# The first matrix of one chunk by seven products on half chunks, on one Trainium2 core

## The chip, the core and the metric

The kernel runs on one core of a Trainium2 chip. The time is the device time of one execution in microseconds. The engines are named as in the profile: PE is TensorE's matmul, PEld its weight load, DVE is VectorE, ACT is ScalarE, POOL is GpSimd, and SP is the engine that issues nearly all transfers (DMAs).

## The reference

```python
# attention: 8 x 8 heads, 576 positions, 64 columns; heads 0 to 3 see the last 32 positions,
# heads 4 to 7 every fourth of the last 128
scores = np.where(masks, scale * np.matmul(q, k.T), -1e9)
attn = np.exp(scores - max); attn = attn / (sum(attn) + 1e-09)
x = np.matmul(attn, v) as (4608 tokens, 512)
# feed-forward
h = x @ w_in                                            # 512 -> 2048
g = np.maximum(h, 0.0) + np.log1p(np.exp(-np.abs(h)))   # softplus
out = g @ w_out                                         # 2048 -> 512
```

All in float32. Each float32 factor is split in a high part, which TensorE multiplies exactly, and a low part, the rest; a product is three matmuls: high by high, high by low, low by high.

## The kernel before

The 4608 tokens are nine chunks of 512. Their inputs x come from attention, which runs for couples of head pairs ahead of the chunk: a visit to PE for the scores, softmax on ACT and DVE, a transposition of 32x32 squares by a way through DRAM, a second visit for the weighted values, and a second way through DRAM that brings x (x_full).

Chunks 0, 1 and 2 are computed directly, in 48 slots (`RUNS`, L43: six slots of chunk 0, ten of chunk 1, ten of 0, six of 1, then all sixteen of chunk 2). A slot is one block of 128 of the 2048 hidden columns: 12 matmuls of 512 columns make its h (`h_part`, L667: 4 blocks of the 512 inputs by three part products, from the weight tile `wt[ff, 0]`), ACT takes the absolute value, exp and ln of it and DVE the maximum (L682 to L689), a cast and a subtraction split it (gh, gl), and two slots later 12 matmuls add it to the four output banks (`o_unit`, L1192; `LAG`, L59).

Chunks 3 to 8 are computed in three pairs ("supers") by Strassen's and Winograd's scheme: both matrices are seen as 2x2 blocks and each 2x2 product is done by seven products instead of eight (`PRODUCTS`, L810), on blocks of one whole chunk (512 columns). The scheme needs sums of blocks on both sides: of x (`x_before`, L996: s1 to s4) and of weights (`job`, L1080: t1 to t4 of one pair of weight tiles p and one matrix i). A job makes its sums on POOL or DVE, splits them, and writes them to DRAM (`streamed`), from where the supers load them into a ring of five tiles. Before, three jobs of the first matrix are done in chunk 0 or 1, seven more jobs during chunk 2, and the last six in the first super.

PE's order is fixed by the order in which `on_tensor` is called, attention visits excepted. Everything else is ordered by a list planner (`planned`, L1471): each task has a cost, a latest time, and a due-time offset from two tables by task number (`HURRIED`, L60, in us, and `CHOSEN`, L68, the engine where there is a choice). At run time each engine works strictly in the order the planner wrote. A tile is used again only once its readers are done, DMAs among them.

Of the kernel before, what the change touches and what calls it, by code (L numbers as in the profile page):

```python
# [53 lines left out]
LATE_JOBS = 6  # L54
# [12 lines left out]
}  # L67
CHOSEN = {  # L68
    295: "ACT", 467: "DVE", 535: "DVE", 554: "DVE", 586: "DVE", 595: "DVE", 819: "DVE", 853: "DVE", 865: "DVE",
    868: "DVE", 882: "DVE", 885: "DVE", 888: "DVE", 901: "DVE", 903: "DVE", 905: "ACT", 908: "DVE", 1210: "DVE",  # L70
    1213: "DVE", 1219: "DVE", 1238: "DVE", 1266: "DVE", 1281: "DVE", 1307: "DVE", 1322: "DVE", 1336: "DVE",
    1345: "DVE", 1580: "DVE", 1670: "DVE", 1676: "DVE", 1694: "DVE", 1716: "DVE", 1731: "DVE", 1767: "DVE",
    1772: "DVE", 1777: "DVE", 2010: "DVE", 2042: "DVE", 2094: "DVE", 2112: "DVE",
# [41 lines left out]
def tile_windowed_attention_softplus_ffn(  # L115
# [22 lines left out]
    opened = const.tile([P, 704], F32, name="opened", tag="k2")  # L138
# [133 lines left out]
    still = opened[:, 448:].bitcast(BF16)  # L272
# [22 lines left out]
    def x_half(c, k):  # L295
        if (c, k) not in x_full:
            turn = k if c < PLAIN else 2 * ((c - PLAIN) % 2) + k
            x_full[c, k] = const.tile([P, 2, CH], F32, name="x_full", tag=f"x_{'abcd'[turn]}")
        return x_full[c, k]
# [412 lines left out]
    def ob_tiles(c, resumed=False):  # L712

        tags = ("w13_0", "w14_0") if c == FIRST else ("x_c", "x_d") if c or not resumed else ("g_x", "g_y", "xl01")
# [106 lines left out]
    def keep_block(i, p, b):  # L821
# [6 lines left out]
        "a11": ("w0_0", "w1_0"), "s2": ("w4_0", "w5_0"), "a12": ("w2_0", "w3_0"), "s3": ("w6_0", "w7_0"),  # L828
        "s1": ("w8_0", "w9_0"), "a22": ("w0_1", "w1_1"), "s4": ("w2_1", "w3_1"),
# [166 lines left out]
    def x_before(c, name):  # L996
        first = c == PLAIN
        if name[0] == "s":
            others = {"s1": ["a22"], "s2": ["s1"], "s3": ["a22", "s2"], "s4": ["s2"]}[name]
            sum_task(1024, x_sum, c, name, reads=[X_KEY[n] for n in others], writes=[X_KEY[name]])  # L1000
        at_home = [k for tag in X_HOMES[name] for k in home_keys(tag)] if first else []
        cast_task(1024, lambda: x_high(c, name), reads=[X_KEY[name]], writes=[("xh", name), *at_home])
        task("DVE", 1024, x_low, c, name, reads=[X_KEY[name], ("xh", name)], writes=[("xl", name)], port=True)
# [13 lines left out]
    def weights(n, begun=False):  # L1017
        x = x_of_couple(n)
        queries = ["q0", "q1"] if begun else [x]
        if not begun:  # L1020
            transfer(load_queries, n, writes=queries, size=TILE, n=2)
# [43 lines left out]
    jobs = {}  # L1065

    def job_tiles(stage):
        if stage not in jobs:
# [7 lines left out]
            tags = (("x_c", "x_d"), ("xl10", "xl11"), ("n3", "n4"))[stage]  # L1076
            jobs[stage] += [tile_at(tag, "cast", F32R, (P, 2, 2, HALF)) for tag in tags]
        return jobs[stage]

    def job(i, p, stage):  # L1080
# [4 lines left out]
        else:  # L1085
            key = [("a", 0), ("a", 1), ("a", 2)]
            key += [("x1", "l", 0), ("x1", "l", 1)] if stage else [("x", 1, 0), ("x", 1, 1)]
            tile_keys = key[:3] if stage == 0 else []
            tile_keys += key[3:]
# [25 lines left out]
        def high(n):  # L1115
            return job_tiles(late)[3 + n][:, :, 0], of(n)

        def low(n):
            dst = job_tiles(late)[3 + n]
# [4 lines left out]
        def keep(n):  # L1124
            for m, b in enumerate(("t2", "t4") if n else ("t1", "t3")):
                load_dma(out=streamed[i, b, p // 2][:, p % 2], in_=job_tiles(late)[3 + n][:, m].bitcast(F32))
# [49 lines left out]
    def early_slot(i):  # L1176
# [9 lines left out]

    OB_KEYS = {
        "kept": [("x", 1, 0), ("x", 1, 0), ("x", 1, 1), ("x", 1, 1)], 0: [("gx",), ("gy",), ("x0", "l", 1), ("x0", "l", 1)],
        1: [("x", 1, 0), ("x", 1, 0), ("x", 1, 1), ("x", 1, 1)], 2: [("W", 13, 0), ("W", 13, 0), ("W", 14, 0), ("W", 14, 0)],
    }  # L1190

    def o_unit(i):  # L1192
# [7 lines left out]
        for m in range(NKT):  # L1200
# [3 lines left out]
        if not final:  # L1204
            return
# [211 lines left out]
    last_resumed = slots.index((2, 0)) + LAG  # L1417
    for i in range(PLANNED, LAST + 1):
        if i == kept_first + 1:
            for n in range(FIRST_JOBS):  # L1420
                sooner(job, JOBS_SOONER)(n // NPAIR, n % NPAIR, 0)
        if slots[i] == (2, 0):
            for k in range(2):
                cast_task(1024, lambda k=k: x_half_high(2, k), reads=[("x", 0, k)], writes=[("x0", "h", k)])
                task(
                    "DVE", 1024, x_half_low, 2, k, reads=[("x", 0, k), ("x0", "h", k)], writes=[("x0", "l", k)], port=True
                )
# [228 lines left out]
```

## Time and profile before

| | |
|---|---|
| median of three executions | 818.75 us (816.95 to 819.33) |
| the profiled execution | 819.88 us, its span 818.1 us |
| PE busy | 801.9 us, 98% of the span |
| DVE busy | 660.2 us, 81% |
| ACT busy | 501.8 us, 61% |
| POOL busy | 189.4 us, 23% |
| DMA | 268 GB/s in the mean |

The span runs from the first to the last instruction; the profiled execution takes 1.8 us more than it. A busy PE is one with a matmul in its pipeline, so that the space between the starts of matmuls tells more than the busy share. Times in rows count from the start of the span. In this profile chunk 2 begins at 224.75 us, its last output matmul ends at about 327.65 us, where the first super begins. A line of a row can be that of a helper: L237 is every matmul, L940 every sum, L972 and L974 every copy and cast on ACT and on DVE.

### The profile page before, as it was taken

How to read it: one execution, taken by the hardware profiler on the slowest of the kernel's cores; microseconds unless marked ns; L12 is line 12 of the kernel's file. 1: busy time of each engine (PE TensorE's matmuls, PEld its weight loads, DVE VectorE, ACT ScalarE, POOL GpSimd, SP SyncE). 2: the span in 40 equal slices, each digit the busy share in tenths (PEclk: the TensorE clock that was granted, in tenths of full speed). 3: DMA queues.
4: the chain of work that ended last, by engine and by line, in shares of the span. 5: the costliest groups of instructions: out<-in, count | busy, mean ns of one | idle time of the engine just before them, and what ended most of it. 6: DMA issues, size and time to landing. Idle time of an engine off the chain costs nothing.

```text
span 818.1 us, 19668 instructions
## 1 busy us (share of the span) xinstructions
PE 801.9 (98%) x7833; PEld 654.2 (80%) x7835; DVE 660.2 (81%) x967; ACT 501.8 (61%) x1122; POOL 189.4 (23%) x132
## 2 busy tenths in 40 slices
PE   6999999999999999999999999999999999999998
PEld 4678888788888888888787888888888888888886
DVE  4798899957687766897999887897997846778974
ACT  5787788745666645596786413889943616775410
POOL 0000000054043324754313202202024302221510
PEclk9699999999999999999999999999999999999999
DMA  9774999968879673999988999879989675556573
GB/s 298 242 242 129 307 374 339 314 208 287 278 249 296 210 219 142 374 336 357 350 295 303 316 352 333 289 240 346 298 269 308 233 248 189 196 190 199 189 218 140
DMA packets 118490, 218.94 MB, mean 268 GB/s; under 512 B 11520, under 2 KB 53632, under 8 KB 118400
## 3 DMA queue, kind: packets, MB, share of 16 engines
q1 hardware_dynamic: 117968, 216.97, 79.1%
q8 instruction: 62, 1.02, 0.5%
q10 hardware_dynamic: 432, 0.72, 0.3%
q14 instruction: 28, 0.23, 0.1%
HBM read 162.07 MB, written 55.57 MB: 266 GB/s over the span
## 4 chain that ended last, share of the span: by engine, by line
PE 72%; DVE 10%; DMA 9%; ACT 5%; issue 2%; POOL 1%; SPq 0%; POOLq 0%; DVEq 0%; ACTq 0%
PE y L237 20%; PE z L237 12%; PE x L237 12%; PE h_ps L237 11%; PE o_ps L237 10%; PE a_ps L237 3%; DMA raw<-w 3%; PE s_ps L237 3%; DMA w_t<-cast 2%; ACT s L433 2%; ACT e L1308 1%; DVE g_of L940 1%; DVE a L216 1%; DMA v<-vp 1%; DMA k<-kdl 1%
## 5 line engine op out<-in xcount | busy, mean ns | idle before, releaser
L940 POOL TENSOR_TENSOR g_of<-g_of 128x1024 f32<-128x1024 f32 x33 | 80.3, 2434 | 258.6 <-DVE g_of L1311 133.3
L940 DVE TENSOR_TENSOR g<-g_of,g 128x1024 fp32r<-128x1024 f32 x84 | 121.3, 1450 | 15.0 <-ACT g L972 14.5
L237 PE MATMUL o_ps<-gh,parts 128*128 128x512 f32 x384 | 129.2, 394 | 0.0
L237 PE MATMUL h_ps<-xh,parts 128*128 128x512 f32 x384 | 129.1, 394 | 0.0
L972 ACT CAST g<-g_of 128x1024 fp32r<-128x1024 f32 x61 | 63.9, 1051 | 102.8 <-PE z L237 44.3
L1308 ACT ACTIVATE e<-e 128x1024 f32<-128x1024 f32 x96 | 101.1, 1058 | 1.7
L237 PE MATMUL y<-g,ring 128*128 128x512 f32 x432 | 100.5, 390 | 0.0
L237 PEld LDWEIGHTS y<-g,ring 128*128 128x128 f32 x432 | 80.8, 188 | 17.1
L940 POOL TENSOR_TENSOR b<-parts 128x512 f32<-128x512 f32 x29 | 40.4, 1393 | 213.5 <-DVE parts L231 143.8
L237 PEld LDWEIGHTS h_ps<-xh,parts 128*128 128x128 f32 x384 | 72.4, 188 | 15.6 <-DVE x_full L587 0.4
L237 PEld LDWEIGHTS o_ps<-gh,parts 128*128 128x128 f32 x384 | 72.1, 188 | 15.9
L433 ACT ACTIVATE s<-s,nm 128x64 f32<-128x64 f32 x224 | 74.8, 336 | 7.2 <-DVE nm L424 7.1
L237 PE MATMUL h_ps<-xl,parts 128*128 128x512 f32 x192 | 75.0, 391 | 0.0
L237 PE MATMUL o_ps<-gl,parts 128*128 128x512 f32 x192 | 74.8, 390 | 0.0
L237 PE MATMUL z<-g,ring 128*128 128x512 f32 x288 | 66.7, 390 | 0.5 <-DVE g L940 0.5
L237 PE MATMUL x<-g,ring 128*128 128x512 f32 x288 | 66.5, 390 | 0.0
L237 PE MATMUL z<-s_h,ring 128*128 128x512 f32 x192 | 63.3, 390 | 0.7 <-DVE temp L940 0.7
L237 PE MATMUL y<-s_h,ring 128*128 128x512 f32 x192 | 63.6, 392 | 0.3 <-DVE temp L940 0.3
L237 PEld LDWEIGHTS z<-g,ring 128*128 128x128 f32 x288 | 53.9, 188 | 12.1 <-DVE g L940 0.9
L237 PE MATMUL x<-a_h,ring 128*128 128x512 f32 x192 | 63.3, 390 | 0.0
L237 PEld LDWEIGHTS x<-g,ring 128*128 128x128 f32 x288 | 53.9, 188 | 11.5 <-DVE g L940 0.2
L940 DVE TENSOR_TENSOR g_of<-y,temp 128x512 f32<-128x512 f32 x60 | 39.6, 682 | 28.7 <-PE y L237 28.6
(111 smaller groups left out, 1522.4 us busy)
## 6 DMA issues: line engine op xcount, KB each, us to landing
ring<-w_t SPq DMA_DIRECT2D x96, 512.0 KB, 4.7
ring<-w_b SPq DMA_DIRECT2D x72, 512.0 KB, 5.1
raw<-w SPq DMA_DIRECT2D x64, 256.0 KB, 5.6
w_t<-cast SPq DMA_DIRECT2D x64, 256.0 KB, 5.5
w_b<-parts SPq DMA_DIRECT2D x48, 256.0 KB, 5.1
v<-vp SPq DMA_DIRECT2D x14, 512.0 KB, 5.7
x_full<-vp SPq DMA_DIRECT2D x14, 512.0 KB, 5.8
turned<-sq SPq DMA_DIRECT2D x112, 64.0 KB, 3.2
```

The source lines that it names most:

```text
L216: pin(nc.vector.scalar_tensor_tensor(out=ai, in0=low, scalar=29, in1=ai, op0=ALU.logical_shift_right, op1=ALU.bitwise_or,))
L237: last_matmul[0] = tc.keep_in_program_order(nc.tensor.matmul(**kw))
L433: pin(nc.scalar.activation(out=self.blocks[:, t], in_=src, func=AF.Exp, bias=self.nm[:, t : t + 1], scale=1.0 / 8.0 if self.masked else 1. ...
L940: pin((nc.gpsimd if name == "POOL" else nc.vector).tensor_tensor(out=dst, in0=a, in1=b, op=op))
L972: pin(nc.scalar.copy(out=dst, in_=src))
L1308: pin(nc.scalar.activation(out=to(), in_=of(), func=func, **kw))
```

## The change

The first matrix of chunk 2 is now computed by the seven products too, on halves of the chunk (256 tokens). A pair of slots (two weight tiles) becomes seven products of six matmuls of 256 columns each, in place of 2 x 12 of 512: for eight pairs 336 matmuls of 256 columns where 192 of 512 stood. The second matrix of chunk 2 stays as it was; its matmuls are laid between the products, one group of three behind each.

- The weights' sums of the first matrix are made one pair at a time, and the products of chunk 2 read them in the tile where they were split (`cast_of`), beside the transfer that keeps them for the supers. So all eight jobs of the first matrix now lie in chunk 2, the three early jobs are of the second matrix, and five are left for the first super (`LATE_JOBS`).
- x of chunk 2 is split in seven blocks of 128x512 (`half_before`): four sums, seven casts, seven subtractions, where two casts and two subtractions of 128x1024 stood.
- Seven products need sums behind them (`half_after`): per pair two copies and five additions of 128x256 out of the banks, then the same softplus, its absolute value and its maximum in halves.
- Two products' results lie side by side in one bank (`REGION`: x and z in one, y in the other).
- The second half of a pair is ready after the sixth product, the first after the seventh; the output matmuls of a slot lie up to a pair later than before.
- Some tiles have other homes, the attention visits lie elsewhere, and both tables have new numbers.

PE, chunk 2's first product and what surrounds it. Before, a slot is (names: xh and xl are the high and low part of x, parts a weight tile, o_ps an output bank, gh and gl the split hidden values):

```order
L237 MATMUL o_ps_2968<-gh,parts 128x512
L237 MATMUL h_ps<-xh,parts 128x512
L237 MATMUL h_ps<-xl,parts 128x512
L237 MATMUL h_ps<-xh,parts 128x512 x2
L237 MATMUL h_ps<-xl,parts 128x512
```

Now the same place holds the first two products of the first pair (cast is the tile with a job's split sums):

```order
L247 MATMUL o_ps_2891<-gh,parts 128x512
L247 MATMUL h_ps<-xh,parts 128x256
L247 MATMUL h_ps<-xl,parts 128x256
L247 MATMUL h_ps<-xh,parts 128x256 x2
L247 MATMUL h_ps<-xl,parts 128x256
L247 MATMUL h_ps<-xh,parts 128x256
L247 MATMUL o_ps_2874<-gh,parts 128x512
L247 MATMUL o_ps_2874<-gl,parts 128x512
L247 MATMUL o_ps_2874<-gh,parts 128x512
L247 MATMUL h_ps<-xh,cast 128x256
L247 MATMUL h_ps<-xl,cast 128x256
```

Each h matmul has half the columns, and three output matmuls lie between two products; the second product waits for a job's tile.

PE, the first attention visit of the weighted values that the planner places (a_ps, between chunk 0's slots). Before:

```order
L237 MATMUL o_ps_2211<-gh,parts 128x512
L237 MATMUL o_ps_2211<-gl,parts 128x512
L237 MATMUL o_ps_2211<-gh,parts 128x512
L237 MATMUL a_ps<-v,sq 32x64 x32
L237 MATMUL a_ps<-x_full,sq 32x64 x32
L237 MATMUL o_ps_2220<-gh,parts 128x512
```

Now, in the output unit of the same slot:

```order
L247 MATMUL o_ps_2239<-gh,parts 128x512
L247 MATMUL o_ps_2239<-gl,parts 128x512
L247 MATMUL o_ps_2239<-gh,parts 128x512
L247 MATMUL a_ps<-v,sq 32x64 x32
L247 MATMUL a_ps<-x_full,sq 32x64 x32
L247 MATMUL h_ps<-xh,parts 128x512
```

The visit stood behind the first of the unit's four groups of three (the bank o_ps_2211, now 2216) and stands behind the fourth: nine matmuls of 512 columns later.

DVE in the middle of chunk 2, a stretch of its list now (part is a tile of the partial results, gl and cast the low parts, s and nm the softmax):

```order
L951 TENSOR_TENSOR part<-h_ps,part 128x256
L951 TENSOR_TENSOR b<-parts 128x512
L985 COPY part<-h_ps 128x256
L430 SCALAR_TENSOR_TENSOR s<-s_ps,mask 128x512
L435 TENSOR_REDUCE nm<-s 128x8
L430 SCALAR_TENSOR_TENSOR s<-s_ps,mask 128x512
L435 TENSOR_REDUCE nm<-s 128x8
L1361 SCALAR_TENSOR_TENSOR e<-part,e 128x256 x4
L951 TENSOR_TENSOR part<-h_ps,part 128x256 x2
L985 CAST a_h<-x_full 128x1024
L715 TENSOR_TENSOR gl<-e,gh 128x512
```

The additions out of the banks stand in line behind softmax steps and casts of the next chunk. From the last maximum of chunk 1 to chunk 2's last low part DVE's list now has 197 instructions: 90 of 128x256, 83 of 128x512 (reductions counted here), 2 of 128x1024, 6 casts and 16 small ones. In the profile of before DVE has 117 in chunk 2's stretch.

The diff without the two tables, the new homes of tiles and the parts that only pass keys:

```diff
-LATE_JOBS = 6
+LATE_JOBS = NPAIR - FIRST_JOBS
...
 HURRIED = {
-    18: -46, 57: -2, 80: 8, 81: -22, 173: -2, 179: -36, 180: -16, 183: 28, 198: -30, 295: 30, 338: -16, 554: -4,
+    2: -24, 7: 32, 11: -94, 31: -74, 41: -46, 50: -22, 71: 34, 85: -28, 195: -38, 210: -72, 295: 30, 450: -20,
...
+def stage_of(p):
+    return 1 if p % 2 and p > 2 else 3
...
+def cast_of(stage, n):
+    if (stage, n) not in casts:
+        tag = (("x_c", "x_d"), ("xl10", "xl11"), ("n3", "n4"), ("xh10", "xh11"))[stage][n]
+        casts[stage, n] = tile_at(tag, "cast", F32R, (P, 2, 2, HALF))
+    return casts[stage, n]
...
+def half_before(name):
...
+    if name[0] == "s":
+        others = {"s1": ["s1", "a22"], "s2": ["s1", "s2"], "s3": ["a22", "s2"], "s4": ["s4", "s2"]}[name]
+        sum_task(512, lambda engine: half_sum(engine, name), ...)
...
+    cast_task(512, lambda: (halves_of(name)[0], half_of(name)), ...)
+    task("DVE", 512, half_low, name, ...)
...
+REGION = {"x": (0, 0), "z": (0, 1), "y": (1, 0)}
...
+def half_unit(p, k):
+    x, name = PRODUCTS[k]
+    b = BANKS[k]
+    if k in (0, 2):
+        regions[REGION[b][0]] = bank("h_ps", "h")
+    xs, m = halves_of(x), 0
+    for kk in range(2):
+        for wp, xp in ((0, 0), (0, 1), (1, 0)):
...
+            matmul(
+                out=region(b), lhsT=lhs, rhs=xs[xp][:, kk], start=k in (0, 2) and m == 0, stop=m == 5,
+                skip_group_check=k not in (0, 2),
+            )
+            m += 1
...
+def paired_slots(i):
+    p = slots[i][1] // 2
+    between = [o_unit(i - LAG - (p > 0), True)]
+    if p:
+        between.append(o_unit(i - LAG, True))
+    for k, (x, name) in enumerate(PRODUCTS):
...
+        on_tensor(3, half_unit, p, k, ...)
+        half_after(i, k, b, [("region", b), bank_key])
+        if k < 4:
+            between[0](k)
+            if p and k == 3:
+                early_split(i - 1)
+        elif p:
+            between[1](k - 4)
+            if k == 6:
+                between[1](3)
+    early_split(i)
...
+def half_after(i, k, b, keys):
+    base = slots[i][1] // 2 % 2 * 4
+    if k == 0:
+        copy_task("ACT", HALF, lambda: (part_of(base), region(b)), reads=keys, writes=[("part", base)])
+        return
+    to, of = {1: (1, base), 2: (2, base), 3: (None, None), 4: (1, 1), 5: (2, 2), 6: (base, base)}[k]
+    if to is not None:
+        task("DVE", HALF, lambda: summed("DVE", part_of(to), region(b), part_of(of), ALU.add), ...)
+    if k == 3:
+        copy_task("ACT", HALF, lambda: (part_of(3), region(b)), reads=keys, writes=[("part", 3)])
+        to = 3
+    if k < 3:
+        return
+    turn, half = {3: (0, 0), 4: (1, 1), 5: (1, 0), 6: (0, 1)}[k]
...
+    task("ACT", HALF, scalar_step, lambda: half_e(i + turn, half), src, AF.Abs, reads=of_keys, writes=[e])
...
+    task("ACT", CH, lambda: scalar_step(whole, whole, AF.Exp, scale=-1.0), writes=[e])
+    task("ACT", CH, lambda: scalar_step(whole, whole, AF.Ln, bias=1.0), writes=[e])
+    for source, read, at in (first_read[turn], (src, of_keys, half)):
+        task("DVE", HALF, rectified, source, at, reads=read, writes=[e], port=True)
...
         if i == kept_first + 1:
             for n in range(FIRST_JOBS):
-                sooner(job, JOBS_SOONER)(n // NPAIR, n % NPAIR, 0)
+                sooner(job, JOBS_SOONER)(1, n, 0)
         if slots[i] == (2, 0):
...
+            for name in ORDER:
+                half_before(name)
             couples(2 * NPAIR - 4, 2 * NPAIR)
-            for n in range(FIRST_JOBS, 2 * NPAIR - LATE_JOBS):
-                sooner(job, JOBS_SOONER)(n // NPAIR, n % NPAIR, 1)
-        early_slot(i)
-        if i == last_resumed:
+        if slots[i][0] < FIRST:
+            early_slot(i)
+        elif i % 2 == 0:
+            p = slots[i][1] // 2
+            sooner(job, JOBS_SOONER)(0, p, stage_of(p))
+            paired_slots(i)
+        if i == weights_gone:
             couples(2 * NPAIR, 2 * NPAIR + 4)
```

## Rows read from the trace of the kernel before

**Rows 1.** The page's first part: busy us, share of the span, instructions.
```profile
PE 801.9 (98%) x7833; PEld 654.2 (80%) x7835; DVE 660.2 (81%) x967; ACT 501.8 (61%) x1122; POOL 189.4 (23%) x132
```
**Rows 2.** Busy us of each engine by stretch, then PE's clock, DMA share, GB/s.
```profile
13.20:13.90 0.70, 0.70 (x20) 0.58 (x6) 0.22 (x1) 0.52 (x4) 0.00 (x0) 1.00 1.03 403
28.30:29.60 1.30, 1.30 (x5) 0.72 (x3) 1.00 (x3) 0.69 (x2) 0.00 (x0) 0.50 0.83 239
224.75:327.65 102.90, 102.75 (x1177) 84.08 (x1176) 76.31 (x117) 60.38 (x162) 37.06 (x35) 1.00 0.70 223
340.00:440.00 100.00, 98.49 (x1155) 79.64 (x1154) 90.11 (x136) 79.26 (x170) 40.96 (x35) 1.00 0.94 331
```
**Rows 3.** PE's waits from 340 to 440 us: total us, times, longest.
```profile
PE z L237 <- DVE temp L940: 0.7, 1, 0.7
PE z L237 <- DVE g L940: 0.5, 1, 0.5
PE y L237 <- DVE temp L940: 0.3, 1, 0.3
```
**Rows 4.** The chain of work in order of time: start, us, what.
```profile
224.75 2.72 PE h_ps L237 x12
```
**Rows 5.** Timeline of PE at full clock: start us, us, operation, tile.
```profile
13.25 0.39 PE L237 MATMUL s_ps<-opened 128*128 128x256 bf16 x2
13.48 0.60 PE L464 MATMUL t_ps<-opened,s 128*128 128x128 f32 x4
```
**Rows 6.** The same at half clock.
```profile
28.78 0.63 PE L237 MATMUL h_ps<-xl,parts 128*128 128x512 f32 x1
29.21 0.63 PE L237 MATMUL h_ps<-xh,parts 128*128 128x512 f32 x1
```
**Rows 7.** Timeline of PEld after a gap in chunk 2.
```profile
300.32 0.19 PEld L237 LDWEIGHTS h_ps<-xh,parts 128*128 128x128 f32 x1 [0.35 <-DVE x_full L587]
300.43 0.19 PEld L237 LDWEIGHTS h_ps<-xl,parts 128*128 128x128 f32 x1
```
**Rows 8.** Groups by shape, DVE and ACT: busy us, mean ns of one, idle before.
```profile
L689 DVE SCALAR_TENSOR_TENSOR e<-h_ps,e 128x512 f32<-128x512 f32 x48 | 32.9, 685 | 29.8 <-ACT e L684 29.4
...
L972 ACT CAST s_h<-x_full 128x1024 fp32r<-128x1024 f32 x11 | 11.6, 1050 | 11.0 <-POOL x_full L940 10.8 <-DVE x_full L940 0.2
...
L620 DVE TENSOR_TENSOR xl<-a_ps,xh 128x256 fp32r<-128x256 f32 x8 | 3.0, 417 | 0.7 <-ACT xh L616 0.7
...
L940 DVE TENSOR_TENSOR x_full<-x_full 128x1024 f32<-128x1024 f32 x2 | 2.4, 1213 | 0.0
```
**Rows 9.** Timeline of DVE, runs of two without a gap.
```profile
29.20 0.75 DVE L620 TENSOR_TENSOR xl<-a_ps,xh 128x256 fp32r<-128x256 f32 x2
...
248.03 1.28 DVE L562 TENSOR_TENSOR normal<-a_ps,ri 128x512 f32<-128x512 f32 x2
```
**Rows 10.** Timeline of PE around the first planned visit of the weighted values.
```profile
154.39 0.39 PE L237 MATMUL o_ps<-gh,parts 128*128 128x512 f32 x1
156.18 0.85 PE L237 MATMUL a_ps<-v,sq 64*32 64x64 f32 x64 [1.40 <-DVE a L207]
```
**Rows 11.** Timeline of PE, ACT and DVE over the last slot of chunk 2.
```profile
319.27 0.39 PE L237 MATMUL h_ps<-xh,parts 128*128 128x512 f32 x1
...
319.69 0.60 ACT L682 ACTIVATE e<-h_ps 128x512 f32<-128x512 f32 x1 [2.08 <-PE h_ps L237]
...
323.11 1.00 DVE L704 TENSOR_TENSOR gl<-e,gh 128x512 fp32r<-128x512 f32 x1 [0.15 <-ACT gh L972]
```
**Rows 12.** Timeline from the last visit for the first super to x's arrival and first sum used.
```profile
296.45 0.96 PE L237 MATMUL a_ps<-x_full,sq 64*32 64x64 f32 x62
...
312.08 1.05 ACT L972 CAST a_h<-x_full 128x1024 fp32r<-128x1024 f32 x1 [1.34 <-DMA x_full<-rows]
...
330.37 0.39 PE L237 MATMUL z<-s_h,ring 128*128 128x512 f32 x1
```

More of the change, by code (lines that the diff above doesn't have):

```diff
@@ L997, in x_before @@
         first = c == PLAIN
+        there = [("W", k, 0) for k in range(2)] if first and name != "s4" else []
         if name[0] == "s":
             others = {"s1": ["a22"], "s2": ["s1"], "s3": ["a22", "s2"], "s4": ["s2"]}[name]
[L1000 removed]
+            sum_task(1024, x_sum, c, name, reads=[X_KEY[n] for n in others] + there, writes=[X_KEY[name]])
         at_home = [k for tag in X_HOMES[name] for k in home_keys(tag)] if first else []
[L1002 to L1003 removed]
+        cast_task(1024, lambda: x_high(c, name), reads=[X_KEY[name], *there], writes=[("xh", name), *at_home])
+        task(
+            "DVE", 1024, x_low, c, name, reads=[X_KEY[name], ("xh", name), *there], writes=[("xl", name)], port=True
+        )
     def x_of_couple(n):
@@ L1075, in job_tiles @@
                 jobs[stage] = job_tiles(0)[:3]
-            tags = (("x_c", "x_d"), ("xl10", "xl11"), ("n3", "n4"))[stage]
-            jobs[stage] += [tile_at(tag, "cast", F32R, (P, 2, 2, HALF)) for tag in tags]
         return jobs[stage]
+    casts = {}
+    def cast_of(stage, n):
[3 more added lines that the diff above has]
+        return casts[stage, n]
     def job(i, p, stage):
@@ L1086, in job @@
             key = [("a", 0), ("a", 1), ("a", 2)]
[L1087 removed]
+            key += [CAST_KEYS[stage](n) for n in range(2)]
             tile_keys = key[:3] if stage == 0 else []
[L1089 removed]
         def flat(j):
@@ L1185, in early_slot, with half_of, halves_of @@
         task("DVE", 512, g_low, i, reads=[e, gh], writes=[gl], port=True)
+    halves, parted = {}, []
+    def half_of(name):
+        r, k = X_HALF[name]
+        return x_half(FIRST, k)[:, :, r * HALF : (r + 1) * HALF]
+    def halves_of(name):
+        if name not in halves:
+            r, k = X_HALF[name]
+            if name in HALF_TAGS:
+                both = const.tile([P, 2, CH], F32R, name=name, tag=HALF_TAGS[name][0])
+                halves[name] = [both[:, :, n * HALF : (n + 1) * HALF] for n in range(2)]
+            elif name == "s4":
+                halves[name] = [gpool.tile([P, 2, HALF], F32R, name=name, tag=tag) for tag in ("g_x", "g_y")]
+            else:
+                halves[name] = [part[k][:, :, r * HALF : (r + 1) * HALF] for part in x_tiles(FIRST)]
+        return halves[name]
@@ new lines, in part_of, with half_e @@
+    def part_of(n):
+        if not parted:
+            two = gpool.tile([P, 2, HALF], F32, name="part", tag="pt")
+            more = gpool.tile([P, 2, HALF], F32, name="part", tag="t2")
+            other = gpool.tile([P, HALF], F32, name="part", tag="p0")
+            parted.extend([two[:, 0], two[:, 1], more[:, 0], more[:, 1], other])
+        return parted[n]
+    def half_e(i, half):
+        if i not in ready:
+            ready[i] = epool.tile([P, CH], F32, name="e")
+        return ready[i][:, half * HALF : (half + 1) * HALF]
@@ L1199, in o_unit, with part @@
             transfer(ob_tiles, c, True, reads=["kept"], writes=sorted(set(keys)), size=TILE * 2, n=4)
-        for m in range(NKT):
+        def part(m):
             on_tensor(
@@ L1203, in o_unit, with o_finished @@
             )
-        if not final:
-            return
+            if final and m == NKT - 1:
+                o_finished(i, resumed, keys)
+        if by_part:
+            return part
+        for m in range(NKT):
+            part(m)
+    def o_finished(i, resumed, keys):
+        c, ff = slots[i]
         for m in range(NKT):
```

129 lines of the change are left out of this document (102 added, 27 removed), and 18 rows, old and new, of the table HURRIED.

## The prediction

> **What bounds the kernel now.** I read the page's busy shares first, then the busy time by stretch, then the waits and the chain. PE is busy for 98% of the span [rows 1], and in chunk 2's stretch for 102.75 of 102.90 us, with DVE at 74% (76.3 us) [rows 2]. So there the time is the sum of PE's matmuls, and only fewer or quicker ones, or a new wait, change it. The reader should then see how quick one is, from the space between starts: the chain has 12 matmuls of 512 columns in 2.72 us, 0.2267 us each [rows 4]. From 340 to 440 us, in the first super, DVE is busy for 90% [rows 2] and PE waits for it three times, 0.7 + 0.5 + 0.3 = 1.5 us [rows 3]. That stretch is my measure of what a full DVE costs PE.
>
> **The products.** Removed: 16 slots x 12 = 192 matmuls of 512 columns, 192 x 0.2267 = 43.5 us. Added: 8 pairs x 7 products x 6 = 336 of 256 columns. No row shows one of these with 4-byte operands, so I bound it. Below: two bf16 matmuls of 256 columns, each with its own weights, take 0.23 us from the first start to the next instruction's [rows 5], 0.115 each, at full clock (1.00, the 2.4 GHz level) [rows 2]; half of 0.2267 is 0.113. Above: if what a 512-column matmul takes beyond its columns is paid per matmul. At half clock (0.50, 1.2 GHz [rows 2]) two starts lie 0.43 us apart [rows 6], 0.84 ns a column, so at full clock 512 columns are 0.213 us and 0.0134 is left; 256 columns would take 0.107 + 0.013 = 0.120. That no such rest shows at half clock speaks for a limit per column (0.113); that PE loads new weights for each, for one per matmul. The load matters more here: it must fit behind 256 columns. After a gap two loads of 128x128 start 0.11 us apart [rows 7], though each is shown as 0.19 long; so it just fits. If loads did not lie behind the matmul's last part at all, but a load and the rest came in series, it would be 0.11 + 0.013, with the matmul's start between them about 0.129; and if the 0.19 shown were the true spacing, 0.188. I take 0.117, between 0.113 and 0.120: 336 x 0.117 = 39.3 us, a gain of 4.2. Ends: 0.113 gives 5.5; 0.129 gives 0.2; 0.188 loses 19.7. The page TensorE: Matmul & The Clock Gate of the Trainium skill, in its section Back-to-back issue gap, gives N/2.4 + 2.5 ns for an isolated warm matmul: 109 ns for 256 columns, 336 x 0.109 = 36.6 us and a gain of 6.9, so 2.7 more than my term. For 512 columns it gives 216 ns where these rows show 226.7, so the measurement decides and I do not use it.
>
> **The attention visit.** At 154.39 us PE starts an output matmul and the next thing, the visit, starts at 156.18 [rows 10]. One matmul takes 0.23, so about 1.56 us are lost, once. (The row names a DVE instruction that has nothing to do with the visit; the squares come by DMA.) In the new order the visit stands nine matmuls later, 9 x 0.2267 = 2.04 us of other work, more than the wait. If the squares land when they did, the wait is gone: -1.5. It could also be moved on by a later transfer: 0.
>
> **DVE in chunk 2.** This is the cost of the change. Per pair five additions and two copies of 128x256 come, the maxima are in halves, and x needs more sums. The list has 197 instructions where the stretch had 117 [rows 2]. A run of two shows what one costs in line: 128x512, 1.28 - 0.68 = 0.60 us; 128x256, 0.75 - 0.42 = 0.33 us [rows 8, 9]. So: 90 x 0.333 + 83 x 0.60 + 2 x 1.13 + 6 casts x 0.37 + 16 small x 0.13 = 30.0 + 49.8 + 2.3 + 2.2 + 2.1 = 86.4 us at the least. PE needs in the same stretch 39.3 (products) + the output units (18 lie in the stretch, 17 of them before the last low part's end: 17 x 2.72 = 46.3 [rows 4]) + 7 attention visits of about 1.53 us (busy for 0.85 and 0.96 in their two halves, which overlap [rows 10, 12]) = 10.7: 96.3 us. DVE is at 90%, the share of 340 to 440 us. There PE lost 1.5 us in 100: I take +1.5. The tight places are the additions out of the y region: the third, fifth and seventh product write it, and between them lie 3 output matmuls, one product and 3 more, 2 x 0.68 + 0.70 = 2.1 us, in which an addition of 0.42 us must come to its turn behind up to three instructions of 0.6. In the first pair no output matmuls lie behind the fifth and sixth product: 0.70 us there. Ends: 0, if the order leaves the gaps where they are needed; above, DVE does not run in line but at each instruction's mean (90 x 0.417 + 83 x 0.685 + 2.4 + 3 + 2.6 = 102.4 us), 6.1 us more than PE has, and with the tenth of its time that it idles in its densest stretch, some 10 more: 16.
>
> ACT gets 16 halves more and up to two copies a pair; at 60.4 of 102.9 us [rows 2] it hides them. POOL loses work. The weights' sums: eight jobs where seven stood in the stretch, and their tiles are needed by a given product; the reading product waits if a job is late, which I count in the term above. The transfer that keeps a tile must land before the tile's next use, one pair or 11.5 us later (two thirds of the pairs; else two), and SP's queue holds attention's transfers too.
>
> **The end of chunk 2.** The last seventh product ends, then come 2 groups of output matmuls (1.36) and the unit of the slot before last but one (2.72): 4.08 us until the last but one's hidden values are wanted. Before, from the last h matmul's end, 319.49 (0.23 after 319.27), through ACT's start at 319.69 to the end of the low part at 324.11, it took 4.6 us [rows 11]. The new chain has an addition more, and the low part is wanted 0.23 us later than the high one: 4.7 against 4.1, +0.6 (0 to 1.5).
>
> **The first super's x.** The last visit now stands before the last pair, 7 x 0.70 + 8 x 0.68 + 3 x 2.72 + 2.72 = 21.2 us ahead of the matmul that first reads a sum of x; it was 330.37 - 297.41 = 33.0 [rows 12]. On the way x took 312.08 - 297.41 = 14.7 us to arrive, then a sum (1.21 on DVE), a cast (1.05) and a subtraction (1.21) follow [rows 8], with hops some 18.5. It fits with 2.7 to spare: 0 (up to +3). The five late jobs, one fewer, are off PE's path: 0; the 1.5 us of waits after 340 us may go (-1.5) or stay; I leave them.
>
> **The sum.** -4.2 - 1.5 + 1.5 + 0.6 = -3.6 us. The profiled execution is 819.88 us (span 818.1 and 1.8 around it), so 816.3; it lies 1.1 above the median of 818.75, so the forecast against the median is 815.2 us.
>
> **The rivals.**
> - DVE becomes the bound of chunk 2. For it: 90% at the least, single-buffered regions of a bank, additions behind softmax steps of 0.6 us. Against: the stretch from 340 us is as full and loses 1.5. Midway between its two ends, 6.1 and 16, PE would wait some 9 us in place of 1.5: 815.2 + 7.5 = 822.7. It makes the kernel slower by more than can be told once chunk 2's waits pass 4.2 + 1.5 + 2.5 - 0.6 = 7.6 us.
> - The weights are not hidden. At 0.129 the products give back 4.0: 819.2, no change to be told. At 0.188 the kernel takes 815.2 + 23.9 = 839. Against the latter: two loads 0.11 apart [rows 7].
> - x for the first super is late. SP's queue issues in order, and with chunk 2 3 us shorter the same transfers have less time; one more delay of 5 to 6 us on the way makes PE wait 3: 818.2.
> - All is covered: 0.113 a matmul, no new wait (-1.5 - 0.6 against the sum): 815.2 - 1.3 - 2.1 = 811.8.
>
> **How the numbers follow.** A change of under 0.3%, 2.5 us, can't be told from none here: faster is under 816.3, slower over 821.2. Forecast 0.45, its own range 813 to 817.5; DVE the bound 0.15; 0.129 0.07 and 0.188 0.03; late x 0.15; all covered 0.15. Four fifths of the forecast and all of "covered" are faster: 0.36 + 0.15 = 0.51. A fifth of the forecast, late x and 0.129 are no change: 0.09 + 0.15 + 0.07 = 0.31. DVE and 0.188 are slower: 0.18. The range 811.5 to 821.5 leaves out most of the DVE case, 0.188 and a little below "covered", 0.2 in all.
>
> **What would show it.** The space between starts in a product: 0.113 to 0.120. DVE's busy share in chunk 2: about 90%, and PE's waits on part, gh or gl there: about 2 us in all, one of them in the first pair or at the end. No wait of the visit near 156 us. The first super's first sum product without a wait for x. The forecast is wrong if chunk 2's waits exceed 5 us, if the space is 0.125 or more, or if the time saved in chunk 2 comes back as new waits after it.

## The result and the profile after

The changed kernel takes 830.59 us, the median of 6 runs (826.51 to 831.91). The kernel before, in its 6 runs, takes 818.05 (816.71 to 820.96). The ratio is 1.0143, with a 95% interval of 1.0114 to 1.0173: some 12 us slower, where 815.2 was forecast in a range up to 821.5. The profiled execution of the changed kernel took 831.91 us, with a span of 830.1.

I cut both spans at two matmuls, the first of chunk 2 and the first of the first super. In the kernel before, the former starts at 224.59 us; the 224.75 used so far is where the chain of work puts its row. "scores_later" is the changed kernel with one visit put back (first experiment).

| stretch, us | before | after | scores_later | after - before | forecast |
|---|---|---|---|---|---|
| start to chunk 2 | 224.59 | 226.56 | 222.23 | +1.97 | -3.0 |
| chunk 2 | 103.06 | 112.87 | 109.54 | +9.81 | -0.6 |
| the rest | 490.41 | 490.68 | 490.89 | +0.27 | 0 |

One attention visit of 1.5 us has moved from the first stretch into chunk 2; the forecast's terms are split accordingly (-1.5 - 1.5, and -4.2 + 1.5 + 0.6 + 1.5). Each column is one execution, and the start differs from one to the next: the scores' visit that stands at 101.73 us in the kernel before and at 99.88 in the changed one begins between 99.2 and 102.4 in the profiles of the changed kernel and its variants below.

The page's first part (busy us, share of the span, instructions) and two stretches (duration, then busy us and instructions of PE, PEld, DVE, ACT and POOL, PE's granted clock, DMA share, GB/s) answer [rows 1, 2]:

```profile
PE 799.0 (96%) x7977; PEld 656.5 (79%) x7979; DVE 673.8 (81%) x1046; ACT 510.2 (61%) x1156; POOL 173.8 (21%) x121
```
```profile
117.30:123.30 6.00, 0.66 (x3) 0.21 (x3) 5.71 (x11) 5.94 (x23) 0.00 (x0) 0.77 1.07 379
226.56:339.43 112.87, 105.77 (x1449) 90.31 (x1448) 93.52 (x200) 72.98 (x232) 18.01 (x21) 0.98 0.77 251
```

Two things are new. In chunk 2 PE is busy for 105.77 of 112.87 us, where it was 102.75 of 102.90: it now stands idle for 7 us. And from 117.3 to 123.3, long before chunk 2, PE is busy for 0.66 of 6 us. The waits of PE over the whole run (total us, times, longest), those that are new from 100 us to the first super, say on what:

```profile
PE s_ps L247 <- DMA k<-kdl: 6.5, 2, 5.4
PE a_ps L247 <- DMA sq<-turned: 3.4, 1, 3.4
PE o_ps L247 <- DVE gl L715: 1.9, 3, 1.2
PE h_ps L247 <- DVE part L985: 1.0, 1, 1.0
PE h_ps L247 <- DVE part L951: 0.6, 2, 0.3
```

Of the first, 5.4 us are the pause at 117 us, where an attention visit that computes scores waits for its keys; the rest lies at the start. The other four lie in chunk 2, 6.9 us together.

**The products.** The timeline of PE at the first product (start, us, operation):

```profile
226.56 0.28 PE L247 MATMUL h_ps<-xh,parts 128*128 128x256 f32 x1
226.68 0.28 PE L247 MATMUL h_ps<-xl,parts 128*128 128x256 f32 x1
...
227.28 0.40 PE L247 MATMUL o_ps<-gh,parts 128*128 128x512 f32 x1
```

Between the first and the last of these rows lie the product's six matmuls: 0.72 us, 0.119 to 0.120 each. So 336 take 40.0 us, and the gain is 43.5 - 40.0 = 3.5, where 4.2 was forecast. The output matmuls between the products start about 0.235 us apart, not 0.227; over all 216 that takes some 0.9 back.

**What chunk 2 would take with no wait.** Before: 43.5 (products) + 216 x 0.2267 = 49.0 (outputs) + 6 visits x 1.5 = 101.5, so 1.56 of its 103.06 us were lost. After: 40.0 + 49.0 + 7 x 1.5 = 99.5, so 13.37 of 112.87 are lost. In scores_later it is 10.04 of 109.54. This puts the 12 us between the two spans together: -3.5 (products), -1.6 (the wait near 156 us, which is gone), +6.9 (the keys' pause), -1.9 (the start: 99.88 against 101.73), +3.3 (what chunk 2 has beyond scores_later's), +8.5 (scores_later's 10.04 less 1.56), +0.3 (rest): 12.0. The pause's 6.9 is what the way from the visit at 100 us to chunk 2 takes more (126.68 against 122.86), with the visit of 1.5 and the wait of 1.6 that are gone from it added.

**The pause at 117 us.** PE in the changed kernel, as before, with the wait in brackets:

```profile
117.57 0.39 PE L247 MATMUL h_ps<-xh,parts 128*128 128x512 f32 x1
123.31 2.04 PE L247 MATMUL s_ps<-k,x_full 64*32 64x64 f32 x128 [5.35 <-DMA k<-kdl]
...
125.88 0.63 PE L247 MATMUL o_ps<-gl,parts 128*128 128x512 f32 x1
126.30 1.05 PE L247 MATMUL o_ps<-gh,parts 128*128 128x512 f32 x2
```

SP's queue in the changed kernel (start of issue, time of issue), then in the kernel before, and there the visit on PE:

```profile
108.39 9.83 SPq L174 DMA_DIRECT2D w_b<-parts  x12
118.31 1.36 SPq L174 DMA_DIRECT2D k<-kdl  x2
```
```profile
112.14 9.59 SPq L164 DMA_DIRECT2D w_b<-parts  x12
121.82 1.34 SPq L164 DMA_DIRECT2D k<-kdl  x2
...
130.61 1.51 PE L237 MATMUL s_ps<-k,x_full 64*32 64x64 f32 x128
```

In both kernels the keys stand behind twelve stores of plain weight blocks (w_b), each of which takes 0.8 us to issue. Before, the keys are issued at 121.82 and PE comes to the visit at 130.61, without a wait. After, PE comes to it at about 117.8, before the keys are issued at all: in the new order of PE the visit stands 48 matmuls of 512 columns, 48 x 0.2267 = 10.9 us, earlier than in the old one. The visit itself then takes 2.04 us where it took 1.51, and the starts behind it come 0.59 us and three times 0.427 apart and not 0.227: the granted clock is 0.50 from 123.30 to 125.35, the 1.2 GHz level, and 0.61 in the mean from there to 127.90.

**The pause in chunk 2.** The visit of the weighted values for the third couple in the changed kernel, and what PE does behind it:

```profile
247.98 0.86 PE L247 MATMUL a_ps<-v,sq 64*32 64x64 f32 x64
252.22 0.86 PE L247 MATMUL a_ps<-x_full,sq 64*32 64x64 f32 x64 [3.38 <-DMA sq<-turned]
...
255.23 0.63 PE L247 MATMUL o_ps<-gh,parts 128*128 128x512 f32 x1
255.66 0.63 PE L247 MATMUL o_ps<-gl,parts 128*128 128x512 f32 x1
```

The second half of the visit waits 3.38 us for its squares. From 253.95 to 257.22 starts are 0.43 us apart (0.21 with 256 columns), the 1.2 GHz level (granted clock 0.53 in the mean): ten matmuls of 256 columns and three of 512 take 3.27 us in place of 1.87, 1.4 more. With 6.9 us of waits that is 8.3 of the 13.4 lost. No row shows the other 5 us as a wait. Found in the starts are the slower outputs (0.9), restarts (up to 1.8, last section), and starts that come later than the row's wait says, as in the next rows.

**The end of chunk 2 and what follows.** The last low part, where [rows 11] stood:

```profile
333.21 0.63 PE L247 MATMUL o_ps<-gh,parts 128*128 128x512 f32 x2
334.07 0.50 PE L247 MATMUL o_ps<-gl,parts 128*128 128x512 f32 x1 [0.22 <-DVE gl L715]
334.40 0.63 PE L247 MATMUL o_ps<-gh,parts 128*128 128x512 f32 x2
```

Two matmuls from 333.21 should end in a start at 333.66; it comes at 334.07, 0.4 late, where the row shows 0.22. All waits of PE from 335 us to the end:

```profile
PE x L247 <- issue: 1.5, 1, 1.5
PE s_ps L247 <- issue: 0.8, 1, 0.8
PE y L247 <- DVE cast L1145: 0.4, 1, 0.4
```

None is at the first super's start, so x arrives in time. They sum to 2.7 us, against 1.5 before [rows 3].

### The profile page after: what moved, and what is told of

Same layout as the page of the kernel before. It is cut to its first block, busy times and chain, and to the rows that moved or that the text cites. A ratio compares the mean times of both kernels' runs of the same rounds, so it can differ in the third digit from the quotient of the medians.

```text
span 830.1 us, 20068 instructions
## 1 busy us (share of the span) xinstructions
PE 799.0 (96%) x7977; PEld 656.5 (79%) x7979; DVE 673.8 (81%) x1046; ACT 510.2 (61%) x1156; POOL 173.8 (21%) x121
## 4 chain that ended last, share of the span: by engine, by line
PE 86%; DMA 5%; DVE 4%; ACT 2%; issue 2%; SPq 1%; DVEq 0%; ACTq 0%
PE y L247 24%; PE x L247 16%; PE z L247 16%; PE o_ps L247 12%; PE h_ps L247 12%; PE s_ps L247 3%; PE a_ps L247 3%; DMA raw<-w 3%; SPq L174 1%; DMA q<-qp 1%; DMA sq<-turned 1%; ACT s L444 1%; DMA k<-kdl 1%; DVE gl L715 0%; DVE part L951 0%
## 5 line engine op out<-in xcount | busy, mean ns | idle before, releaser
L951 POOL TENSOR_TENSOR g_of<-g_of 128x1024 f32<-128x1024 f32 x39 | 93.7, 2404 | 232.7 <-DVE g_of L1510 93.2
L247 PE MATMUL o_ps<-gh,parts 128*128 128x512 f32 x384 | 136.2, 397 | 0.0
L983 ACT CAST g<-g_of 128x1024 fp32r<-128x1024 f32 x59 | 62.0, 1053 | 112.3 <-PE y L247 43.9
L247 PE MATMUL h_ps<-xh,parts 128*128 128x512 f32 (+1 forms) x320 | 101.6, 374 | 0.1
L951 POOL TENSOR_TENSOR b<-parts 128x512 f32<-128x512 f32 x22 | 28.7, 1309 | 223.5 <-DVE parts L241 154.1
L247 PEld LDWEIGHTS h_ps<-xh,parts 128*128 128x128 f32 x320 | 59.4, 189 | 11.6 <-DVE part L951 0.5
L247 PE MATMUL h_ps<-xl,parts 128*128 128x512 f32 (+1 forms) x160 | 59.1, 370 | 0.0
```

The lines of the kernel that those rows point to most:

```text
L247: last_matmul[0] = tc.keep_in_program_order(nc.tensor.matmul(**kw))
L951: pin((nc.gpsimd if name == "POOL" else nc.vector).tensor_tensor(out=dst, in0=a, in1=b, op=op))
L983: pin(nc.scalar.copy(out=dst, in_=src))
```

## The experiments

Three theories of the loss. **Keys**: the visit that stands too early on PE, or its keys too late on SP, costs most of it. **DVE's work**: chunk 2 has too much on DVE, the rival that the prediction priced at 9 us. **Order**: what PE wants from DVE, ACT or the queue stands behind something else there; the amount doesn't matter. Most edits move instructions in the finished plan: later(n, m) puts step n, and what depends on it, right behind step m; earlier(n, m) puts n ahead of m. Ratios are to the kernel before, timed beside each group of experiments (its median there lies between 818.2 and 818.9); all medians are in us.

### The keys

scores_later puts the scores' visit back by 48 matmuls. keys_first leaves it and puts the twelve stores behind the keys on SP. before_early goes the other way: in the kernel before, it pulls the visit ahead, with the one maximum on DVE that must precede it.

```diff
+    later(189, 278)
```


> The changed kernel with one visit moved on PE alone: the scores of the second couple of chunk 1 (at 117.6 us, where PE waits 5.5 us for the keys' transfer) stand 48 matmuls of 512 columns later, as in the kernel before. Nothing else moves. Theory A (PE's fixed order asks for visits before their transfers have landed): the 5.5 us and the 0.8 us of half clock behind it go, 830.6 - 6.3 = 824.3 us. Theory B (DVE has too much to do from here to the end of chunk 2, and PE only happens to wait here): what is gained here is waited for later, 828 us or more.

```diff
+    for n in (124, 123, 127, 126, 125, 148, 147, 146, 122, 121, 120, 119):
+        later(n, 188)
```


> The changed kernel with the visit where it is, but on SP's queue the 12 stores of weight parts that stand ahead of those keys' loads are put behind them. Theory A: the keys land before 117.6 us, and the time is that of the kernel with the visit moved, 824 to 825 us. Rival (the DMA engines are full there, share 1.05, so that order on the queue only trades one late transfer for another): the keys land as late, or the stores delay the next visit's squares, 828 us or more.

```diff
+    earlier(173, 254)
+    earlier(189, 261)
```


> The converse, in the kernel before: the same scores visit put 48 matmuls of 512 columns earlier on PE, where the changed kernel has it, and the one maximum on DVE that must precede it put 10 us earlier too; SP's queue as it was. Theory A: PE waits for the keys there as in the changed kernel, 5 to 6 us and 0.8 at half clock: 818 + 6 = 824 us. Theory B: the seven products' DVE work is not there, so what is lost is caught up: 819 us or less.

Measured: scores_later 822.51 (ratio 1.0037, 1.0017 to 1.0057), keys_first 823.13 (1.0037, 1.0009 to 1.0065), before_early 826.53 (1.0088, 1.0065 to 1.0111). In keys_first SP issues the keys 7.6 us earlier, and PE doesn't wait:

```profile
110.70 1.18 SPq L174 DMA_DIRECT2D k<-kdl  x2
```

In before_early the pause of the changed kernel appears in the old one:

```profile
117.37 0.39 PE L237 MATMUL h_ps<-xh,parts 128*128 128x512 f32 x1
125.00 2.04 PE L237 MATMUL s_ps<-k,x_full 64*32 64x64 f32 x128 [7.24 <-DMA k<-kdl]
```

Two edits with nothing in common but the keys take away 7.5 and 8.1 us of the median, and the same move costs the kernel before 7.6. So the keys are shown as the cause of about two thirds of the loss. Of chunk 2, too, 3.3 us seem to go with them: it takes 109.54 in both mended kernels, and the stretch in scores_later (as above) and its longest waits are

```profile
222.23:331.77 109.54, 104.39 (x1450) 88.94 (x1448) 93.31 (x200) 73.03 (x232) 18.05 (x21) 1.00 0.79 257
```
```profile
PE o_ps L247 <- DVE gl L715: 1.9, 3, 1.2
PE a_ps L247 <- DMA sq<-turned: 1.6, 1, 1.6
...
```

The squares' wait is half as long, and the clock is 1.00 in the mean. But thin_max below, its keys mended too, shows 2.8 us of wait for the squares and a chunk 2 of 112.20 in the one execution that was profiled, so that the keys alone set this part is not shown. DVE's three waits are the same to the tenth (1.9, 1.0 and 0.6). 10 us of chunk 2 are left to explain; the next kernels start from scores_later.

### The wait near 156 us

before_values moves the visit of [rows 10] back by some nine matmuls in the kernel before, as the change does.

```diff
+    later(200, 356)
```


> The kernel before, with the one visit that waits 1.56 us for its squares at 154 us moved nine matmuls of 512 columns later on PE, as the changed kernel has it. Theory A (a visit waits only as long as its transfers need, and other work in its place is a gain): -1.5 us, 816.7 us. Rival (the squares are used that much later, and the next steps of attention, or DVE behind the visit, wait in its place): 818.2 us.

817.88 (ratio 0.9986, 0.9969 to 1.0003). In its trace the visit follows on the matmul before it:

```profile
155.22 0.39 PE L237 MATMUL o_ps<-gh,parts 128*128 128x512 f32 x1
155.54 0.86 PE L237 MATMUL a_ps<-v,sq 64*32 64x64 f32 x64
```

The wait is gone, as forecast; of its 1.5 us 1.0 shows in the median, and this is not told apart from none.

### The amount of DVE's work

thin_max takes the maxima on 8 of 256 columns. thin_dve also takes sums out of the banks (from the third pair on) and most low parts of the weights' sums on 8 columns. Both so leave hidden values unfinished; the order is as it was.

```diff
-                out=half_e(i + turn, half), in0=of(), scalar=0.0, in1=half_e(i + turn, half), op0=ALU.max, op1=ALU.add
+                out=half_e(i + turn, half)[:, :8], in0=of()[:, :8], scalar=0.0, in1=half_e(i + turn, half)[:, :8], op0=ALU.max, op1=ALU.add
```


> The kernel with the scores visit 48 matmuls later (822.5 us); the 32 maxima of half a block in chunk 2 work on 8 columns in place of 256, so that part of the hidden values is left without its maximum. DVE has some 8 us less to do in chunk 2, in the same order. Theory B: PE's waits for DVE, about 5 us, go: 817.5 us. Theory C: only those directly behind maxima go (0.3 to 0.5 us in two pairs): 821.5 us.

```diff
...
+            w = HALF if slots[i][1] // 2 < 2 else 8
...
-                "DVE", HALF, lambda: summed("DVE", part_of(to), region(b), part_of(of), ALU.add),
+                "DVE", HALF, lambda: summed("DVE", part_of(to)[:, :w], region(b)[:, :w], part_of(of)[:, :w], ALU.add),
```


> The kernel with the scores visit later (822.5 us), with DVE's work in chunk 2 made small: all maxima, the sums out of the banks from the third pair on, and six of the eight jobs' low parts work on 8 columns, so that these hidden values and sums are left unfinished. DVE has some 20 us less to do of 86, in the same order. Theory B: the waits for DVE, 5 us, go, and chunk 2 takes 103 us or less. Theories C and D (order, shared bank, transfers that hold a tile): pairs 1 and 2 lose what they lost, and only pairs 4 and 5 gain: chunk 2 takes 106 to 109 us.

thin_max 821.32 (1.0051, 1.0023 to 1.0080), thin_dve 821.01 (1.0030, 1.0010 to 1.0050): neither is told from scores_later. The profiled execution of thin_max took 829.74, 8.4 more than its median, so I don't weigh its chunk 2 against the others. The stretch of thin_dve, and its longest wait there:

```profile
220.29:327.17 106.88, 102.94 (x1449) 89.19 (x1448) 72.88 (x199) 72.79 (x232) 18.10 (x21) 1.00 0.81 266
```
```profile
PE o_ps L247 <- DVE gl L715: 1.5, 2, 1.2
...
```

DVE is busy for 72.88 us where it was 93.31, and less than in the kernel before [rows 2]. Chunk 2 becomes 2.7 us shorter, not 10, and the long waits stay: the theory of DVE's work holds for about a quarter. The mean share hides how full DVE is where PE loses most. Pairs two to six, in scores_later and then in thin_dve:

```profile
231.66:300.17 68.51, 63.59 (x978) 53.57 (x971) 62.47 (x134) 47.93 (x162) 16.76 (x20) 1.00 0.83 278
229.73:296.28 66.55, 62.61 (x976) 53.86 (x972) 49.87 (x135) 48.45 (x163) 16.80 (x20) 1.00 0.86 284
```

DVE is busy for 91% of these pairs and then for 75%, and the time falls by 2.0 us; by the sum above PE loses 8.8 us in them in scores_later, so some 6.9 stay.

### The order

Where does DVE stand when PE wants its first late gl? The timeline of DVE in scores_later:

```profile
236.95 0.75 DVE L951 TENSOR_TENSOR part<-h_ps,part 128x256 f32<-128x256 f32 x2 [0.39 <-PE h_ps L247]
237.62 1.28 DVE L1423 TENSOR_TENSOR ob<-o_ps,ob 128x512 f32<-128x512 f32 x2
238.81 0.68 DVE L951 TENSOR_TENSOR b<-parts 128x512 f32<-128x512 f32 x1
239.41 0.68 DVE L715 TENSOR_TENSOR gl<-e,gh 128x512 fp32r<-128x512 f32 x1
```

and PE behind it:

```profile
240.15 0.50 PE L247 MATMUL o_ps<-gl,parts 128*128 128x512 f32 x1 [1.19 <-DVE gl L715]
```

Two additions and a sum stand ahead of the low part; without these 1.8 us it would have been in time. dve_order puts such low parts, and some sums and copies out of banks, ahead of what is not urgent. squares_ahead sends the second squares of the visit near 248 us ahead of two stores of weights' sums and the loads of queries on SP, and fetches them ahead of the next couple's loads. both_visits puts that visit itself back. mended joins dve_order and squares_ahead, and in the first super sends one ring load ahead of a late job's stores.

```diff
+    later(523, 721)
```


> The changed kernel with the scores visit 48 matmuls later as above, and the first visit of chunk 2 for weighted values (at 248 us, 3.4 us of wait for its second squares, then 1.9 us at half clock) moved 9 matmuls of 512 and 12 of 256 columns later, 3.4 us of work. Theory A: 824.3 - 5.3 = 819 us. Theory B: the squares are late because DVE and the transfers behind it are late, so that PE waits for gl and part in its place: 823 us or more.

```diff
+    later(595, 508)
+    later(669, 508)
+    later(647, 509)
+    later(531, 509)
```


> The kernel with the scores visit 48 matmuls later (822.5 us), and on SP's queue alone the second set of squares of chunk 2's first couple is sent before two transfers of weight sums and one of queries, and fetched before the loads for the next couple; PE, DVE and ACT as they were. Theory A (the visit at 244 us waits 1.6 us because its squares stand behind other transfers in SP's order): the wait goes, 821 us. Theory B (chunk 2 ends when DVE's list ends, as the end of chunk 2 at 330.3 to 331.8 us in three kernels that began it at 219.5, 220.8 and 222.2 suggests): PE waits for part and gl a little longer in its place, 822.5 us.

```diff
+    earlier(607, 604)
+    earlier(588, 615)
+    later(615, 614)
...
+    earlier(867, 864)
```


> The kernel with the scores visit 48 matmuls later (822.5 us), and eleven instructions of DVE in chunk 2 change places: in two pairs the sum out of bank y stands before that out of bank x-z; two low parts stand before work that is wanted later; in one pair a sum and a copy out of the banks stand before two transpositions and a sum of weights. The same instructions, as many. Theory C (PE waits because what it needs stands in DVE's list behind what it does not need, and because x and z share a bank, so that a sum of z waits for the product of x): the waits of 0.4, 1.35, 0.65, 0.5, 1.15 and 0.3 us go, 818.5 us. Theory B (DVE's work in chunk 2 is the bound, whatever its order): 822 us.

```diff
+    later(1071, 1344)
+    later(1074, 1344)
```


> The scores visit 48 matmuls later, the squares ahead and DVE's new order together, and in the first super one load of weights on SP's queue stands before the two transfers of a late job that wait for DVE (PE waited 1.3 us at 393 us). If A and C hold and add up: 822.5 - 1.6 - 4 - 1.3 = 815.6 us, less than the kernel before. If B holds: 821 us.

| kernel | median | ratio (95%) | chunk 2 |
|---|---|---|---|
| scores_later | 822.51 | 1.0037 (1.0017 to 1.0057) | 109.54 |
| both_visits | 824.19 | 1.0074 (1.0044 to 1.0104) | 112.28 |
| squares_ahead | 822.30 | 1.0057 (1.0038 to 1.0077) | 110.13 |
| dve_order | 825.53 | 1.0083 (1.0055 to 1.0112) | 110.77 |
| mended | 827.00 | 1.0101 (1.0066 to 1.0137) | 109.82 |

Each takes its wait away or shortens it, and none is told faster than scores_later. The longest waits of squares_ahead in chunk 2, then of dve_order:

```profile
PE h_ps L247 <- DVE part L951: 2.4, 4, 1.7
...
```
```profile
PE a_ps L247 <- DMA sq<-turned: 2.9, 1, 2.9
PE o_ps L247 <- DVE gl L715: 1.2, 4, 0.6
...
```

With the squares in time, PE comes to the next product sooner and waits 1.7 us for its part. With gl earlier, it comes to the squares sooner and waits 2.9 for them. In both_visits DVE, in its list's order, stands 4.19 us at the visit's result, and PE then waits 2.69 us for a sum that is queued behind it:

```profile
247.00 0.69 DVE L573 TENSOR_TENSOR normal<-a_ps,ri 128x512 f32<-128x512 f32 x1 [4.19 <-DMA w_t<-cast]
252.66 1.53 PE L247 MATMUL h_ps<-s,cast 128*128 128x256 f32 x6 [2.69 <-DVE part L951]
```
(The releaser in the first row has nothing to do with a_ps; DVE waited for the visit that was moved back.)

In squares_ahead ACT shows a wait that PE's rows don't name, at the casts of the weights' sums, 1.17 us at one and 2.35 at the next:

```profile
249.50 0.62 ACT L983 CAST cast<-b 128x512 fp32r<-128x512 f32 x1 [2.35 <-DMA out_t<-ob]
250.15 0.69 DVE L1145 TENSOR_TENSOR cast<-b,cast 128x512 fp32r<-128x512 f32 x1 [2.12 <-ACT cast L983]
251.57 0.98 PE L247 MATMUL h_ps<-s,cast 128*128 128x256 f32 x6 [1.68 <-DVE part L951]
```

A cast must wait until the last transfer out of the tile that it overwrites has landed. In these two it is the transfer of chunk 1's outputs, which lie in the same tiles (`xl10`, `xl11`); in one more, 1.44 us at 237.88, it is that of the sums of the pair before. Behind ACT stands DVE, and behind DVE PE: this is the 1.7 us wait for a part. Three kernels put these casts later (with the edits of squares_ahead and dve_order): casts_later by most, casts_mid by less, and best_try, on casts_later, puts two softmax steps of DVE behind sums out of the banks.

```diff
+    later(710, 629)
+    later(758, 733)
+    later(761, 737)
```


> The kernel with the scores visit later, the squares ahead and DVE's new order (no change in the first super), and three casts of weight sums moved behind work that does not wait: in the traces so far ACT stands at these casts for 0.9, 1.1 and 2.1 us until a transfer out of the tile that the cast overwrites has landed (the sums of the pair before, the outputs of chunk 1), DVE's low parts stand behind ACT, and PE behind DVE. Theory D (the tiles of the weight sums are reused before their transfers out have landed, which holds up ACT and DVE in their order): pairs 1 and 2 of chunk 2, which lost 4.9 us, lose about 1.5: 3.4 us less than the kernel without this, some 819 us. Theory B (DVE's work is the bound): the loss stays, 822 us or more.

```diff
+    later(710, 629)
+    later(761, 729)
+    later(758, 729)
```


> As the kernel with the casts later, but two of the three casts are moved back: behind the copy and the two casts of hidden values that ACT has next, not 5 us further, since PE waited 4.6 us for them at 257.6 us. Theory D: pair 3 loses 0.5 us in place of 7.6, pairs 1 and 2 about 3.2 as there, chunk 2 takes some 107.5 us, and the time is 820.5 us. Theory B: chunk 2 takes 109.5 us or more.

```diff
+    later(654, 819)
+    later(677, 867)
```


> As the kernel with the casts later, and in pairs 4 and 5 of chunk 2 two softmax steps of DVE stand behind the sums out of the banks. Theory C and D together: pairs 4 and 5 lose 1 us in place of 3.4 as well, some 817 us, about the kernel before. Theory B: no gain over the kernel with the casts later.

casts_later 827.38 (1.0097, 1.0058 to 1.0135; chunk 2 114.89), casts_mid 822.52 (1.0045, 1.0026 to 1.0064; 110.53), best_try 829.53 (1.0123, 1.0090 to 1.0156; 116.04). In casts_later PE's longest wait is 4.4 us, for ACT's copy of a part that stands behind the casts: put too late, they stop PE. At the middle place ACT no longer waits at the casts, and PE waits 2.2 us for DVE's sum.

### The way the weights are read

plain_blocks tries one more rival: that the new tile of sums and its layout delay PE. It reads the plain blocks in place of the sums' tile, and so leaves the sums out of the hidden values.

```diff
-                    lhs = cast_of(stage_of(p), n)[:, at, wp, kk * P : (kk + 1) * P]
+                    lhs = wt[2 * p + n, 0][:, wp, at * HALF + kk * P : at * HALF + (kk + 1) * P]
```


> The kernel with the scores visit later (822.5 us), where the products that read a job's sums read the plain weights in their place: the hidden values of chunk 2 are wrong, the jobs are done and sent as before, and PE waits for none of them. Theory E (the sums, used where they are made, set the pace: a product waits for a job, or a job for a product that still reads its tile): pairs 1 and 2 lose 1.5 us or less in place of 4.9, and the time is 819 us. Theories C and D: PE hardly waits for the sums themselves, and the loss stays within 0.7 us: 822 us.

824.27 (1.0060, 1.0039 to 1.0082), chunk 2 109.77. DVE's waits are those of scores_later, 1.9, 1.0 and 0.6; the rival falls.

## Why the prediction was wrong

- **The products: right in kind, 0.7 too much.** 0.119 us and not 0.117, within the range given. So what a matmul costs beyond its columns is paid by each one (0.0134 by [rows 4, 6], 0.12 in all), and its weight load lies behind it. The 0.9 us that the outputs between the products take more had no term.
- **The attention visit: the step that failed first.** "If the squares land when they did, the wait is gone: -1.5. It could also be moved on by a later transfer: 0." The wait near 156 us did go. But I looked at that visit alone. The change gives the planner other tasks and new tables and so moves nearly all visits: the scores' visit of the second couple went 10.9 us ahead on PE, while its keys stayed behind the same twelve stores on SP. No term of the sum held this, though both orders showed it before any run. It costs 7.5 to 8.1 us by the medians of three kernels, and 6.9 by the profile.
- **DVE in chunk 2: the step that failed second.** "There PE lost 1.5 us in 100: I take +1.5." Chunk 2 lost 10.0 us with the keys mended and 13.4 as it is, where it had lost 1.6. The size is the rival's, 9 us, but its mechanism, too much work, carries about a quarter: with 20 us less work on DVE the loss falls by 2.7. The share of 90% was right where it matters (91% in pairs two to six of scores_later; 93.52 of 112.87, 83%, over chunk 2 of the changed kernel). That such a share cost 1.5 us in the first super said nothing on chunk 2, where a product's results are wanted 2 us after it. I named these gaps and then priced them from another stage. At each wait followed above, the traces show one instruction or transfer that stands behind another in an in-order list (DVE, ACT, SP). But PE's rows put only 3.5 us on DVE and 1.6 on the squares, and no order tried gave any of the 10 us back: that the order is their cause is argued, not shown.
- **One bank, two accumulations.** In the row of 236.95 us DVE waits 0.39 us for PE on h_ps: the halves for x and for z lie in one bank, and the program makes the sum of one wait for the last matmul of the other: z's product had started its last matmul at 233.76, and DVE starts right after the next product for x, whose last one starts at 236.56. I had taken the regions as independent, as the planner does. The Trainium skill, PSUM — Partial Sum Buffer, section Terms, says that two engines on one bank and quadrant at once are an error. The trace shows the wait alone; no run here has the halves in two banks, so what this costs PE stays open.
- **The end of chunk 2**: 0.4 us where 0.6 was forecast. **The first super's x**: no wait, as forecast. **After 340 us**: 2.7 us of waits for 1.5, and the stretch is 0.3 longer.

What stays open: what gives the 10 us of chunk 2 back, another order, two banks for x and z, or tiles of their own for the casts. Every wait that was taken away let another one show, and no version is faster than the kernel before; 817.88 (before_values) is not told from it.

## What to carry to other kernels

Where a planner sets the order, compare the place of every visit, load and store in both orders, engine by engine, above all on a queue that issues in order, and not only at the place that the change is about: here a visit moved ahead by 10.9 us while its load kept its place, and that cost 7 to 8. A busy share measured in one stage is no price for another: count how long after each result is made it is wanted, and what stands ahead of its instruction in its engine's list. And one wait taken out of a chain of waits gives back what is left to the next one, not its own length.

## What was not expected of the hardware

- A matmul with 4-byte operands of 256 columns starts every 0.119 us with new weights for each, so 0.238 for 512 columns in two halves, against 0.2267 in one.
- After a wait or an attention visit the first start is about 0.1 us longer: 334.07 to 334.40 is 0.33 us for one matmul of 512 columns that else takes 0.227. In chunk 2 there are 17 such places, up to 1.8 us that no row shows as waits; the kernel before has seven.
- After the pause of 5.35 us the visit and the first four starts behind it were at the 1.2 GHz level at once. After that of 3.38 us the first starts were at full pace, and half pace came from 253.9 to 257.1. After 1.6 us, in scores_later, the mean over chunk 2 is 1.00.
- A store of 256 KB of plain weight blocks holds SP's queue for 9.83 / 12 = 0.82 us while the DMA share is 1.07; twelve of them hold back a load behind them by 9.8 us.
